# Attention and MLP on one core: turning q, k and the attention's rows by DMA instead of on TensorE

## The chip, the cores and the metric

The kernel runs on one NeuronCore of a Trainium2 chip. The metric is the device time of one execution in microseconds (us); times compared are medians of several runs. The engines are named as in the profile: PE is TensorE (matrix multiplication), PEld its weight loads, DVE is VectorE, ACT is ScalarE, POOL is GpSimd and SP is SyncE, which here only issues DMAs.

## The reference

Softmax attention over 8 batches, 12 heads, 448 positions, 64 columns per head; the heads' results stand side by side as rows of 768 columns; a two-layer MLP with a leaky ReLU follows.

```python
batch, n_heads, seq, head_dim = (8, 12, 448, 64)
scores = scale * np.matmul(q, k.transpose(0, 1, 3, 2))        # scale = 1 / sqrt(64)
attn = np.exp(scores - np.max(scores, axis=-1, keepdims=True))
attn = attn / (np.sum(attn, axis=-1, keepdims=True) + 1e-09)
attn_out = np.matmul(attn, v)
x = attn_out.transpose(0, 2, 1, 3).reshape(B * S, H * D)      # 3584 rows of 768
h = x @ w_in                                                  # w_in 768 x 2048
g = np.maximum(0.01 * h, h)
return g @ w_out                                              # w_out 2048 x 768
```

Inputs and output are float32; the kernel multiplies in bf16.

## The kernel before

Two heads make a **pair**; there are 48 pairs, numbered u, six in a batch. A pair's q, k and v are 448 rows, held as 112 partitions with four rows each (SC = 112, NSC = 4), two heads of 64 columns beside each other, so that a block of 112 partitions has 128 columns.

For each pair these functions run:

- `load(u)`: three DMAs from SP's queue bring q, k and v (224 KB each) into the buffers fq, fk, fv; the pool `ld` holds six pairs.
- `cast(u)`: POOL turns them into bf16: tiles q and k, and v into one of five v tiles.
- `transposes(u)`: eight PE transposes of 112 x 128 blocks (four of q, four of k) into the PSUM tile tr, and one DVE copy (L154) to qkT, of which there are three. qkT has the 128 columns of both heads on its partitions, and first q's, then k's 448 positions in the free dimension.
- `scores(u, c)`: two matmuls into PSUM (sc) for each of four groups of 112 keys; `expo(u, c)`: ACT's exponential to the tile e.
- `pv(u, j)`: sixteen matmuls for each head, with a column of ones in v that gives the sum; DVE divides (L188, L189) and writes bf16 rows x.
- `x_transposes(u)`: four PE transposes of x into tr and one or two DVE copies (L202) to xT, whose partitions are columns of the MLP's input and whose free dimension is its rows.

The MLP runs over eight groups of rows, `cuts` = 0, 384, 896, 1280, 1792, 2176, 2688, 3072, 3584, so widths of 384 and 512 alternate. A group's xT is a tile of its own (three in the pool); where a batch's 448 rows cross a cut, they are copied in two pieces. `mlp(i)` multiplies by w_in (96 matmuls, L225, with an activation on ACT to h, L230) and then by w_out (32 matmuls, L237, for each 128 rows, with DVE copies to o, L242, and two stores from SP). It is a generator that yields after each matmul.

The order is written out by hand: nothing is scheduled behind the program's back, each engine runs its instructions in the order of the program, and semaphore waits are set where an instruction needs another's result or buffer. A pair has eight slots s0 to s7 (`slots(u)`): s0 scores of u, s1 `x_transposes(u - 2)`, s2 and s6 pv of u - 1, s3 `load`, s4 scores, s5 `cast(u + 3)` and, early on, a piece of the weights' load on POOL's queue, s7 `transposes(u + 1)`. Between two slots matmuls of `mlp(i)` are put in proportion: `begin[i]` is the slot from which `mlp(i)` is dealt out until `begin[i + 1]`. Whatever is left of a group's MLP is run at its end, and the last group's MLP runs alone. So SP's queue also holds, in the program's order, loads and stores, and a store that waits for its o holds the loads behind it.

```python
begin = [8 * (HP * (i + 1) + 1) + 2 for i in range(B)]
```

Of the kernel before, what the change touches and what calls it, by code (L numbers as in the profile page):

```python
# [10 lines left out]
BF16 = mybir.dt.bfloat16  # L11
# [5 lines left out]
def kernel(  # L17
# [9 lines left out]
    nc = tc.nc  # L27

    B, H, S, D = q.shape
    DM, DF = moe_w_in.shape  # L30
    P = 128
    HP = H // 2
    SC = 112
    NSC = S // SC
    KD = DM // P
    MD = DF // P
    NW = DM // 2
    NU = B * HP
    scale = 1.0 / float(D) ** 0.5

    cuts = [((b * S) // P) * P for b in range(B)] + [B * S]
# [2 lines left out]

    const_pool = ctx.enter_context(tc.tile_pool(name="const", bufs=1))
    w_pool = ctx.enter_context(tc.tile_pool(name="weights", bufs=1))
    ld_pool = ctx.enter_context(tc.tile_pool(name="ld", bufs=6))
    cast_pool = ctx.enter_context(tc.tile_pool(name="cast", bufs=4))
    v_pool = ctx.enter_context(tc.tile_pool(name="vones", bufs=1))
    qk_pool = ctx.enter_context(tc.tile_pool(name="qk", bufs=1))  # L50
    exp_pool = ctx.enter_context(tc.tile_pool(name="exp", bufs=1))
    r_pool = ctx.enter_context(tc.tile_pool(name="rec", bufs=4))
    x_pool = ctx.enter_context(tc.tile_pool(name="x", bufs=3))
    xT_pool = ctx.enter_context(tc.tile_pool(name="xT", bufs=3))
    h_pool = ctx.enter_context(tc.tile_pool(name="h", bufs=2))
    o_pool = ctx.enter_context(tc.tile_pool(name="o", bufs=3))

# [11 lines left out]
    e_sb = [exp_pool.tile([SC, EL + P - SC], BF16, name=f"e{i}") for i in range(NE)]  # L69


    NQ = 3
    QL = 2 * S
    qkT = [qk_pool.tile([P, QL + P - SC], BF16, name=f"qkT{i}") for i in range(NQ)]

    w_in_sb = w_pool.tile([P, KD, DF], BF16)
    w_out_sb = w_pool.tile([P, MD, DM], BF16)
# [1 line left out]
    w_out_v = moe_w_out.rearrange("(ko ki) n -> ki ko n", ki=P)  # L79

    raw = {}
    q_sb = {}
    k_sb = {}

    def load(u, queues=(nc.sync,) * 3):
        if u >= NU:
            return
        b, hp = divmod(u, HP)  # L90
        raw[u] = []
        for a, name, eng in zip((q, k, v), ("fq", "fk", "fv"), queues):
            t = ld_pool.tile([SC, 2, NSC, D], F32, name=name)
            eng.dma_start(
                out=t.rearrange("p h so d -> p h (so d)"),
                in_=a[b, 2 * hp:2 * hp + 2].rearrange("h (p so) d -> p h (so d)", so=NSC),
            )
            raw[u].append(t)

    def cast(u, by=(nc.gpsimd.tensor_copy,) * 3):  # L100
        if u >= NU:
            return
        fq, fk, fv = raw.pop(u)
        q_sb[u] = cast_pool.tile([SC, NSC, 2, D], BF16, name="q")
        k_sb[u] = cast_pool.tile([SC, NSC, 2, D], BF16, name="k")
        by[0](q_sb[u].rearrange("p so h d -> p h so d"), fq)  # L106
        by[1](k_sb[u].rearrange("p so h d -> p h so d"), fk)  # L107
        by[2](v_sb[u % NV][:, :, :, :D], fv)  # L108

    w_steps = []  # L110
# [5 lines left out]
    def load_w(n=1):  # L116
        for _ in range(n):
            if w_steps:
                o, i = w_steps.pop(0)
                nc.gpsimd.dma_start(out=o, in_=i)  # L120

    load(0, (nc.sync, nc.scalar, nc.sync))
    for i in range(1, 6):
        load(i)
    ident = const_pool.tile([P, P], BF16)
    make_identity(nc, ident)
# [10 lines left out]


    x_t = {}
    xT = [None] * (B + 1)  # L140

    def get_xT(i):
        if xT[i] is None:
            xT[i] = xT_pool.tile([P, KD, 4 * P], BF16, name="xT")
        return xT[i]

    def transposes(u):
        tr = ps_tr.tile([P, 2, S], BF16, name="tr")
        for i, src in enumerate((q_sb[u], k_sb[u])):
            for so in range(NSC):  # L150
                nc.tensor.transpose(  # L151
                    tr[:, i, ts(so, SC)], src[:, so], ident[:SC, :SC]
                )
        nc.vector.tensor_copy(qkT[u % NQ][:, :QL], tr.rearrange("p i s -> p (i s)"))  # L154

    sc_t = {}

    def scores(u, c):
        ps = ps_s.tile([P, 2, 512], F32, name="sc")
        t = qkT[u % NQ]  # L160
        sc_t[u, c] = ps
        for j in range(2):
            nc.tensor.matmul(  # L163
                ps[:, j, :S],
                t[j * D:(j + 1) * D, S + c * SC:S + c * SC + P],
                t[j * D:(j + 1) * D, :S],
                start=True, stop=True,
            )

    def expo(u, c):  # L170
        e = e_sb[u % NE][:, :EL].rearrange("p (j c s) -> p j c s", j=2, c=NSC)
        nc.scalar.activation(e[:, :, c, :], sc_t.pop((u, c))[:SC, :, :S], AX.Exp, scale=scale)  # L172

    def pv(u, j):

        e, vt = e_sb[u % NE], v_sb[u % NV]
        ps = ps_pv.tile([P, NSC, D + 1], F32, name="pv")
        for qc in range(NSC):
            for c in range(NSC):
                at = (j * NSC + c) * S + qc * SC  # L180
                nc.tensor.matmul(  # L181
                    ps[:, qc, :], e[:, at:at + P], vt[:, j, c, :],
                    start=(c == 0), stop=(c == NSC - 1),
                )
        if j == 0:
            x_t[u] = x_pool.tile([SC, NSC, 2, D], BF16, name="x")
        rec = r_pool.tile([SC, NSC, 1], F32, name="rec")
        nc.vector.reciprocal(rec, ps[:SC, :, D:])  # L188
        nc.vector.tensor_mul(  # L189
            x_t[u][:, :, j, :], ps[:SC, :, :D], rec.to_broadcast([SC, NSC, D])  # L190
        )

    def x_transposes(u):
        b, hp = divmod(u, HP)
        lo, hi = b * S, (b + 1) * S
        tr = ps_tr.tile([P, 2, S], BF16, name="tr")
        for so in range(NSC):
            nc.tensor.transpose(tr[:, 0, ts(so, SC)], x_t[u][:, so], ident[:SC, :SC])  # L198
        for i in (b, b + 1):
            a, z = max(lo, cuts[i]), min(hi, cuts[i + 1] if i < B else hi)  # L200
            if a < z:
                nc.vector.tensor_copy(  # L202
                    get_xT(i)[:, hp, a - cuts[i]:z - cuts[i]], tr[:, 0, a - lo:z - lo]
                )
        del x_t[u]


    def store(o, t0):

        done = 0  # L210
        while done < P:
            b, j = divmod(t0 + done, S)
            so, p = divmod(j, SC)
            n = min(SC - p, P - done)
            dst = out[b * S:(b + 1) * S].rearrange("(p so) n -> so p n", so=NSC)
            nc.sync.dma_start(out=dst[so, p:p + n], in_=o[done:done + n, :])
            done += n

    def mlp(i):
        n = cuts[i + 1] - cuts[i]  # L220
        h = h_pool.tile([P, MD, 4 * P], BF16, name="h")
        for m in range(MD):
            ps = ps_mm.tile([P, 4 * P], F32, name="mm")
            for kk in range(KD):
                nc.tensor.matmul(  # L225
                    ps[:, :n], w_in_sb[:, kk, ts(m, P)], get_xT(i)[:, kk, :n],
                    start=(kk == 0), stop=(kk == KD - 1),
                )
                if kk == KD - 1:
                    nc.scalar.activation(h[:, m, :n], ps[:, :n], AX.Prelu, alpha=0.01)  # L230
                yield n
        for c in range(n // P):
            o = o_pool.tile([P, DM], F32, name="o")
            for w in range(2):
                ps = ps_mm.tile([P, 4 * P], F32, name="mm")
                for m in range(MD):
                    nc.tensor.matmul(  # L237
                        ps[:, :NW], h[:, m, ts(c, P)], w_out_sb[:, m, ts(w, NW)],
                        start=(m == 0), stop=(m == MD - 1),
                    )  # L240
                    if m == MD - 1:
                        nc.vector.tensor_copy(o[:, ts(w, NW)], ps[:, :NW])  # L242
                    yield NW
            store(o, cuts[i] + c * P)


    def slots(u):

        on = u < NU

        def s0():
            if on:
                scores(u, 0)
                scores(u, 1)
                expo(u, 0)

        def s1():
            if on:
                expo(u, 1)
            if 2 <= u <= NU + 1:  # L260
                x_transposes(u - 2)

        def s2():
            if 1 <= u <= NU:
                pv(u - 1, 0)

        def s3():
            load(u + 6)

        def s4():  # L270
            if on:
                scores(u, 2)
                scores(u, 3)
                expo(u, 2)

        def s5():
            if on:
                expo(u, 3)
            cast(u + 3)
            if u <= 2 or 5 <= u <= 8:  # L280
                load_w()

        def s6():
            if 1 <= u <= NU:
                pv(u - 1, 1)

        def s7():
            if u + 1 < NU:
                transposes(u + 1)

        return [s0, s1, s2, s3, s4, s5, s6, s7]

    steps = [s for u in range(NU + 2) for s in slots(u)]

    begin = [8 * (HP * (i + 1) + 1) + 2 for i in range(B)]
    assert begin[B - 1] == 8 * (NU + 1) + 2
    transposes(0)
    for s in steps[:begin[0]]:
        s()
    for i in range(B):  # L300
        work = steps[begin[i]:begin[i + 1]] if i + 1 < B else []
        n = cuts[i + 1] - cuts[i]
# [42 lines left out]
```

## Time and profile before

| | |
|---|---|
| median of three runs | 460.23 us (457.93 to 462.13) |
| profiled execution, its own time | 456.92 us |
| its span, first to last instruction | 455.2 us |
| granted TensorE clock, mean | 0.998 |
| PE, ACT, DVE, POOL busy | 95%, 51%, 30%, 20% of the span |
| HBM read and written | 45.61 MB and 11.01 MB |
| PE transposes | 576 in three groups: q and k (L151), x (L198) |

Lines such as L151 are lines of the kernel before. A row of a group reads: line, engine, operation, tile written <- tiles read, shapes, count, then busy time in us and the mean duration of one in ns, then the idle time of the engine ahead of it and what ended that. A row of the timeline has the start and the length in us first. In the chain, shares are of the span.

### The profile page before, as it was taken

How to read it: one execution, taken by the hardware profiler on the slowest of the kernel's cores; microseconds unless marked ns; L12 is line 12 of the kernel's file. 1: busy time of each engine (PE TensorE's matmuls, PEld its weight loads, DVE VectorE, ACT ScalarE, POOL GpSimd, SP SyncE). 2: the span in 40 equal slices, each digit the busy share in tenths (PEclk: the TensorE clock that was granted, in tenths of full speed). 3: DMA queues.
4: the chain of work that ended last, by engine and by line, in shares of the span. 5: the costliest groups of instructions: out<-in, count | busy, mean ns of one | idle time of the engine just before them, and what ended most of it. 6: DMA issues, size and time to landing. Idle time of an engine off the chain costs nothing.

```text
span 455.2 us, 9874 instructions
## 1 busy us (share of the span) xinstructions
PE 433.2 (95%) x4143; PEld 248.0 (54%) x4160; DVE 137.8 (30%) x369; ACT 230.6 (51%) x322; POOL 92.1 (20%) x167
## 2 busy tenths in 40 slices
PE   3878999999999999999999999999999999999995
PEld 1545555544556566555555665554556655564463
DVE  1344224422333333332233322342233423340021
ACT  4677663467434675446634476446644376404300
POOL 5536423111221121131111211311221100000000
PEclk9999999999999999999999999999999999999999
DMA  9999996391043810565024460349004110111022
GB/s 233 253 245 275 239 252 189 98 239 39 1 131 97 230 49 1 159 182 133 1 81 127 127 171 2 96 125 249 1 1 131 36 37 2 35 37 35 1 69 69
DMA packets 44332, 50.97 MB, mean 112 GB/s; under 512 B 3328, under 2 KB 40704, under 8 KB 44288
## 3 DMA queue, kind: packets, MB, share of 16 engines
q1 hardware_dynamic: 38800, 43.82, 35.2%
q0 software_dynamic: 5248, 6.29, 7.8%
q8 instruction: 32, 0.52, 0.5%
q10 hardware_dynamic: 240, 0.23, 0.2%
q14 instruction: 12, 0.10, 0.1%
HBM read 45.61 MB, written 11.01 MB: 124 GB/s over the span
## 4 chain that ended last, share of the span: by engine, by line
PE 82%; DMA 13%; DVE 3%; ACT 1%; issue 1%; POOL 0%; POOLq 0%; SPq 0%
PE mm L237 31%; PE mm L225 28%; PE pv L181 9%; PE sc L163 9%; DMA w_out_sb<-in_moe_w_out_dram 4%; PE tr L151 4%; DMA fq<-in_q_dram 4%; DMA fk<-in_k_dram 3%; DVE qkT L154 3%; PE tr L198 2%; DMA fv<-in_v_dram 2%; ACT e L172 1%; POOL v L108 0%; DVE o L242 0%; DVE q L106 0%
## 5 line engine op out<-in xcount | busy, mean ns | idle before, releaser
L172 ACT ACTIVATE e<-sc 112x896 bf16<-112x896 f32 x192 | 167.9, 915 | 126.5 <-PE sc L163 126.2
L237 PE MATMUL mm<-w_out_sb,h 128*128 128x384 bf16 x896 | 166.2, 326 | 0.5 <-DMA w_out_sb<-in_moe_w_out_dram 0.5
L225 PE MATMUL mm<-xT,w_in_sb 128*128 128x384 bf16 (+1 forms) x751 | 164.5, 352 | 0.9
L237 PEld LDWEIGHTS <-h 128*128 128x128 bf16 x896 | 79.5, 97 | 57.9 <-issue 15.1
L230 ACT ACTIVATE h<-mm 128x384 bf16<-128x384 f32 (+1 forms) x128 | 69.8, 545 | 69.7 <-PE mm L225 69.7
L225 PEld LDWEIGHTS <-w_in_sb 128*128 128x128 bf16 x768 | 66.7, 97 | 63.9 <-issue 15.6
L108 POOL CAST v<-fv 112x512 bf16<-112x512 f32 x48 | 29.6, 616 | 239.5 <-PE pv L181 225.9
L181 PEld LDWEIGHTS <-e 112*128 112x128 bf16 x1536 | 62.2, 99 | 15.2 <-issue 1.5
L163 PE MATMUL sc<-qkT 64*128 64x448 bf16 x384 | 56.3, 367 | 10.9 <-DVE qkT L154 6.5
L181 PE MATMUL pv<-v,e 112*128 112x65 bf16 x1536 | 66.2, 195 | 0.0
L242 DVE COPY o<-mm 128x384 f32<-128x384 f32 x56 | 31.2, 557 | 96.8 <-PE mm L237 96.8
L188 DVE RECIPROCAL rec<-pv 112x4 f32<-112x4 f32 x96 | 17.5, 182 | 114.2 <-PE pv L181 114.0
L189 DVE TENSOR_TENSOR x<-pv,rec 112x256 bf16<-112x256 f32 x96 | 40.7, 424 | 3.3
L202 DVE COPY xT<-tr 128x384 bf16<-128x384 bf16 (+1 forms) x72 | 20.3, 309 | 70.9 <-PE tr L198 70.9
L154 DVE COPY qkT<-tr 128x896 bf16<-128x896 bf16 x48 | 29.9, 622 | 23.6 <-PE tr L151 23.5
L163 PEld LDWEIGHTS <-qkT 64*128 64x128 bf16 x384 | 12.1, 95 | 44.5 <-DVE qkT L154 24.7
L106 POOL CAST q<-fq 112x512 bf16<-112x512 f32 x47 | 28.9, 614 | 22.7 <-POOL v L108 13.2
L107 POOL CAST k<-fk 112x512 bf16<-112x512 f32 x47 | 28.9, 614 | 12.8 <-DMA fk<-in_k_dram 9.6
L151 PE MATMUL tr<-ident,q 112*128 112x112 bf16 x192 | 17.9, 217 | 4.8 <-DVE q L106 4.8
L151 PEld LDWEIGHTS <-q 112*128 112x128 bf16 x192 | 14.0, 99 | 11.3 <-DVE q L106 4.8
L198 PEld LDWEIGHTS <-x 112*128 112x128 bf16 x192 | 13.8, 98 | 9.0 <-issue 2.6
L151 PE MATMUL tr<-ident,k 112*128 112x112 bf16 x192 | 17.9, 218 | 0.0
(16 smaller groups left out, 40.1 us busy)
## 6 DMA issues: line engine op xcount, KB each, us to landing
fq<-in_q_dram SPq DMA_DIRECT2D x48, 224.0 KB, 5.5
fv<-in_v_dram SPq DMA_DIRECT2D x48, 224.0 KB, 6.0
fk<-in_k_dram SPq DMA_DIRECT2D x47, 224.0 KB, 6.1
w_in_sb<-in_moe_w_in_dram POOLq DMA_DIRECT2D x4, 768.0 KB, 12.7
w_out_sb<-in_moe_w_out_dram POOLq DMA_DIRECT2D x4, 768.0 KB, 15.9
out_dram<-o SPq DMA_DIRECT2D x8, 336.0 KB, 2.9
out_dram<-o SPq DMA_DIRECT2D x8, 288.0 KB, 2.7
out_dram<-o SPq DMA_DIRECT2D x8, 240.0 KB, 2.7
```

The source lines that it names most:

```text
L106: by[0](q_sb[u].rearrange("p so h d -> p h so d"), fq)
L108: by[2](v_sb[u % NV][:, :, :, :D], fv)
L151: nc.tensor.transpose(tr[:, i, ts(so, SC)], src[:, so], ident[:SC, :SC])
L154: nc.vector.tensor_copy(qkT[u % NQ][:, :QL], tr.rearrange("p i s -> p (i s)"))
L163: nc.tensor.matmul(ps[:, j, :S], t[j * D:(j + 1) * D, S + c * SC:S + c * SC + P], t[j * D:(j + 1) * D, :S], start=True, stop=True,)
L172: nc.scalar.activation(e[:, :, c, :], sc_t.pop((u, c))[:SC, :, :S], AX.Exp, scale=scale)
L181: nc.tensor.matmul(ps[:, qc, :], e[:, at:at + P], vt[:, j, c, :], start=(c == 0), stop=(c == NSC - 1),)
L189: nc.vector.tensor_mul(x_t[u][:, :, j, :], ps[:SC, :, :D], rec.to_broadcast([SC, NSC, D]))
L225: nc.tensor.matmul(ps[:, :n], w_in_sb[:, kk, ts(m, P)], get_xT(i)[:, kk, :n], start=(kk == 0), stop=(kk == KD - 1),)
L230: nc.scalar.activation(h[:, m, :n], ps[:, :n], AX.Prelu, alpha=0.01)
L237: nc.tensor.matmul(ps[:, :NW], h[:, m, ts(c, P)], w_out_sb[:, m, ts(w, NW)], start=(m == 0), stop=(m == MD - 1),)
L242: nc.vector.tensor_copy(o[:, ts(w, NW)], ps[:, :NW])
```

## The change

Pairs 0 to 9 still have q and k turned on PE, and pairs 0 to 6 their x. For the others an SP-issued transposing DMA moves the rows from SBUF to SBUF: one for q and k together, which now stand in one tile qkb, and one for x. The q/k DMA of pair u + 2 is issued in slot s1 of pair u, right behind the x DMA of pair u - 2. There are four qkT instead of three. xT becomes one tile of 4 x 448 = 1792 columns in which four batches follow each other, so a batch's rows are written in one piece. The pool `ld` holds five pairs, and `load` runs five pairs ahead. The MLP of groups 1 to 7 begins five slots later (s7 in place of s2); that of group 0 begins as before and so is dealt out over 53 slots instead of 48.

```diff
-    ld_pool = ctx.enter_context(tc.tile_pool(name="ld", bufs=6))
+    ld_pool = ctx.enter_context(tc.tile_pool(name="ld", bufs=5))
...
-    NQ = 3
+    NQ = 4
...
+    NX = 4 * S
+    xT = xT_pool.tile([P, KD, NX], BF16)
...
-        q_sb[u] = cast_pool.tile([SC, NSC, 2, D], BF16, name="q")
-        k_sb[u] = cast_pool.tile([SC, NSC, 2, D], BF16, name="k")
+        qk_sb[u] = cast_pool.tile([SC, 2, NSC, 2, D], BF16, name="qkb")
...
+    NPE = 10
+
+    def turn(dst, src):
+        nc.sync.dma_start_transpose(out=dst.rearrange("p (c s) -> p c s", s=SC), in_=src)
+
+    def dma_transposes(u):
+        if NPE <= u < NU:
+            turn(qkT[u % NQ][:, :QL], qk_sb[u].rearrange("p i so h d -> p (i so h d)"))
+
     def transposes(u):
+        if u >= min(NPE, NU):
+            return
...
     def x_transposes(u):
         b, hp = divmod(u, HP)
+        at = b * S % NX
+        dst = xT[:, hp, at:at + S]
+        if u >= NPE - 3:
+            turn(dst, x_t.pop(u).rearrange("p so h d -> p (so h d)"))
+            return
...
-                    ps[:, :n], w_in_sb[:, kk, ts(m, P)], get_xT(i)[:, kk, :n],
+                    ps[:, :n], w_in_sb[:, kk, ts(m, P)], xT[:, kk, at:at + n],
...
             if 2 <= u <= NU + 1:
                 x_transposes(u - 2)
+            dma_transposes(u + 2)
...
-            load(u + 6)
+            load(u + 5)
...
-    begin = [8 * (HP * (i + 1) + 1) + 2 for i in range(B)]
+    begin = [8 * (HP * (i + 1) + 1) + 7 - 5 * (i == 0) for i in range(B)]
```

The first place is PE's order where the last pair ends and the last group's MLP begins. Before, x of pair 47 was turned (L198) four matmuls ahead of it; LDWEIGHTS rows are the weight loads of the matmul that follows:

```order
L237 LDWEIGHTS h
L237 MATMUL mm<-w_out_sb,h 128x384
L198 LDWEIGHTS x
L198 MATMUL tr<-ident,x 128x112
...
L237 LDWEIGHTS h
L237 MATMUL mm<-w_out_sb,h 128x384
...
L225 LDWEIGHTS w_in_sb
L225 MATMUL mm<-xT,w_in_sb 128x512
```

And now, behind the last pv of pair 47:

```order
L189 LDWEIGHTS e_112
L189 MATMUL pv<-v_107,e_112 128x65
L244 LDWEIGHTS h
L244 MATMUL mm<-w_out_sb,h 128x384
...
L232 LDWEIGHTS w_in_sb
L232 MATMUL mm<-xT,w_in_sb 128x512
```

The transposes are gone from PE's order, and 36 matmuls of the MLP of group 6 (L244) stand between the last pv and the last group's first matmul (L232).

The second place is SP's queue at the first transposing DMAs. Before, behind the three loads of pair 12, only loads followed for four pairs (in brackets the semaphores that an instruction waits for: DMAHW is a DMA eight places earlier in the queue):

```order
L94 DMA fq<-in_q_dram 112x2x256 [waits DMAHW7_49,Pool_49]
L94 DMA fk<-in_k_dram 112x2x256 [waits DMAHW0_49,Pool_49]
L94 DMA fv<-in_v_dram 112x2x256 [waits DMAHW1_49,Pool_49]
L94 DMA fq<-in_q_dram 112x2x256 [waits DMAHW2_49,Pool_49]
L94 DMA fk<-in_k_dram 112x2x256 [waits DMAHW3_49,Pool_49]
L94 DMA fv<-in_v_dram 112x2x256 [waits DMAHW4_49,Pool_49]
```

And now:

```order
L147 DMA_TRANSPOSE qkT_115<-qkb 128x8x112 [waits DVE_49,DMAHW7_49,PE_49,Pool_49]
L98 DMA fq<-in_q_dram 112x2x256 [waits DMAHW0_49]
L98 DMA fk<-in_k_dram 112x2x256 [waits DMAHW1_49]
L98 DMA fv<-in_v_dram 112x2x256 [waits DMAHW2_49]
L147 DMA_TRANSPOSE xT<-x 128x4x112 [waits DMAHW3_49,DVE_49]
L147 DMA_TRANSPOSE qkT_116<-qkb 128x8x112 [waits DMAHW4_49,PE_49,Pool_49]
L98 DMA fq<-in_q_dram 112x2x256 [waits DMAHW5_49]
```

The loads of pair 13 now stand behind the DMA of q and k of pair 10, which waits for that pair's casts on POOL and for the scores of pair 6 on PE; those of pair 14 stand behind the DMA of x of pair 7, which waits for DVE.

The third place is SP's queue near the end, from the store of the second 128 rows' result of group 6 on. Before:

```order
L216 DMA out_dram<-o 96x768 [waits DMAHW4_49,DVE_49]
L216 DMA out_dram<-o 32x768 [waits DMAHW5_49]
L216 DMA out_dram<-o 80x768 [waits DMAHW6_49,DVE_49]
L216 DMA out_dram<-o 48x768 [waits DMAHW7_49]
L216 DMA out_dram<-o 64x768 [waits DMAHW0_49,DVE_49]
```

And now:

```order
L222 DMA out_dram<-o 96x768 [waits DMAHW2_49,DVE_49]
L222 DMA out_dram<-o 32x768 [waits DMAHW3_49]
L147 DMA_TRANSPOSE xT<-x 128x4x112 [waits DMAHW4_49]
L222 DMA out_dram<-o 80x768 [waits DMAHW5_49,DVE_49]
L222 DMA out_dram<-o 48x768 [waits DMAHW6_49]
```

The DMA of x of pair 47 stands behind two stores, the first of which waits for DVE's copy of a result, and ahead of the store of the third 128 rows.

More of the change, by code (lines that the diff above doesn't have):

```diff
@@ L53 @@
     x_pool = ctx.enter_context(tc.tile_pool(name="x", bufs=3))
-    xT_pool = ctx.enter_context(tc.tile_pool(name="xT", bufs=3))
+    xT_pool = ctx.enter_context(tc.tile_pool(name="xT", bufs=1))
     h_pool = ctx.enter_context(tc.tile_pool(name="h", bufs=2))
@@ L69 @@
     e_sb = [exp_pool.tile([SC, EL + P - SC], BF16, name=f"e{i}") for i in range(NE)]
-    NQ = 3
+    NQ = 4
     QL = 2 * S
     qkT = [qk_pool.tile([P, QL + P - SC], BF16, name=f"qkT{i}") for i in range(NQ)]
+    NX = 4 * S
+    assert all(any(c == d for d in cuts) for c in range(0, B * S + 1, NX))
+    xT = xT_pool.tile([P, KD, NX], BF16)
     w_in_sb = w_pool.tile([P, KD, DF], BF16)
@@ L81 @@
     raw = {}
-    q_sb = {}
-    k_sb = {}
+    qk_sb = {}
     def load(u, queues=(nc.sync,) * 3):
@@ L103, in cast @@
         fq, fk, fv = raw.pop(u)
-        q_sb[u] = cast_pool.tile([SC, NSC, 2, D], BF16, name="q")
-        k_sb[u] = cast_pool.tile([SC, NSC, 2, D], BF16, name="k")
-        by[0](q_sb[u].rearrange("p so h d -> p h so d"), fq)
-        by[1](k_sb[u].rearrange("p so h d -> p h so d"), fk)
+        qk_sb[u] = cast_pool.tile([SC, 2, NSC, 2, D], BF16, name="qkb")
+        by[0](qk_sb[u][:, 0].rearrange("p so h d -> p h so d"), fq)
+        by[1](qk_sb[u][:, 1].rearrange("p so h d -> p h so d"), fk)
         by[2](v_sb[u % NV][:, :, :, :D], fv)
@@ L122 @@
     load(0, (nc.sync, nc.scalar, nc.sync))
-    for i in range(1, 6):
+    for i in range(1, 5):
         load(i)
@@ L139 @@
     x_t = {}
[L140 to L145, printed above, removed]
+    NPE = 10
[4 more added lines that the diff above has]
+            turn(qkT[u % NQ][:, :QL], qk_sb[u].rearrange("p i so h d -> p (i so h d)"))
     def transposes(u):
+        if u >= min(NPE, NU):
+            return
         tr = ps_tr.tile([P, 2, S], BF16, name="tr")
-        for i, src in enumerate((q_sb[u], k_sb[u])):
+        for i in range(2):
             for so in range(NSC):
                 nc.tensor.transpose(
-                    tr[:, i, ts(so, SC)], src[:, so], ident[:SC, :SC]
+                    tr[:, i, ts(so, SC)], qk_sb[u][:, i, so], ident[:SC, :SC]
                 )
@@ L194, in x_transposes @@
         b, hp = divmod(u, HP)
-        lo, hi = b * S, (b + 1) * S
+        at = b * S % NX
[3 more added lines that the diff above has]
+            return
         tr = ps_tr.tile([P, 2, S], BF16, name="tr")
@@ L198, in x_transposes @@
             nc.tensor.transpose(tr[:, 0, ts(so, SC)], x_t[u][:, so], ident[:SC, :SC])
[L199 to L205, printed above, removed]
+        nc.vector.tensor_copy(dst, tr[:, 0, :])
     def store(o, t0):
@@ L220, in mlp @@
         n = cuts[i + 1] - cuts[i]
+        at = cuts[i] % NX
         h = h_pool.tile([P, MD, 4 * P], BF16, name="h")
@@ L293 @@
     steps = [s for u in range(NU + 2) for s in slots(u)]
-    begin = [8 * (HP * (i + 1) + 1) + 2 for i in range(B)]
-    assert begin[B - 1] == 8 * (NU + 1) + 2
+    begin = [8 * (HP * (i + 1) + 1) + 7 - 5 * (i == 0) for i in range(B)]
+    assert begin[B - 1] == 8 * (NU + 1) + 7
     transposes(0)
```

## The prediction

> **What bounds the kernel now.** I read the page from the top: the busy shares, the slices, the chain that ended last.
>
> ```profile
> span 455.2 us, 9874 instructions
> PE 433.2 (95%) x4143; PEld 248.0 (54%) x4160; DVE 137.8 (30%) x369; ACT 230.6 (51%) x322; POOL 92.1 (20%) x167
> DMA  9999996391043810565024460349004110111022
> PE 82%; DMA 13%; DVE 3%; ACT 1%; issue 1%; POOL 0%; POOLq 0%; SPq 0%
> ```
>
> TensorE (PE) is busy for 95% of the span. The DMA engines, in the second line from below, a digit for each slice of 11.4 us, are full for six slices (68 us) and lightly used afterwards. Busy time by stage confirms it (columns: window, then PE, PEld, DVE, ACT, POOL, then granted clock, DMA share, GB/s):
>
> ```profile
> 50.00:60.00 10.00, 9.93 (x97) 5.59 (x96) 2.23 (x6) 7.33 (x13) 2.46 (x4) 1.00 1.14 239
> 90.00:149.00 59.00, 58.73 (x549) 32.48 (x551) 18.54 (x52) 29.42 (x41) 10.73 (x18) 1.00 0.37 98
> 149.00:198.00 49.00, 48.54 (x505) 28.83 (x504) 16.54 (x44) 27.68 (x40) 10.72 (x18) 1.00 0.39 110
> ```
>
> In these windows PE is idle for less than 1% of the time. So an instruction taken off PE shortens the kernel by the time until PE's next one starts, as long as nothing else becomes late. In these stages DMA stands at 0.37 to 0.39 of its capacity and ACT at about half.
>
> **What PE gives up.** The price is the pitch, not the duration. First two groups by shape:
>
> ```profile
> L151 PE MATMUL tr<-ident,q 112*128 112x112 bf16 x192 | 17.9, 217 | 4.8 <-DVE q L106 4.8
> L198 PE MATMUL tr<-ident,x 112*128 112x112 bf16 x192 | 17.6, 215 | 0.0
> ```
>
> Then PE's timeline inside one pair (start, length, what):
>
> ```profile
> 203.00 0.36 PE L151 MATMUL tr<-ident,q 112*128 112x112 bf16 x4
> 203.20 0.36 PE L151 MATMUL tr<-ident,k 112*128 112x112 bf16 x4
> 203.40 1.03 PE L225 MATMUL mm<-xT,w_in_sb 128*128 128x512 bf16 x3
> 204.36 0.55 PE L163 MATMUL sc<-qkT 64*128 64x448 bf16 x4
> ...
> 205.72 0.36 PE L198 MATMUL tr<-ident,x 112*128 112x112 bf16 x4
> 205.91 1.03 PE L225 MATMUL mm<-xT,w_in_sb 128*128 128x512 bf16 x4
> ...
> 214.07 0.55 PE L163 MATMUL sc<-qkT 64*128 64x448 bf16 x4
> ```
>
> A transpose lasts 215 ns, but the first of k starts 0.20 us after the first of q, and the MLP's matmul 0.20 us after that: the eight of q and k occupy PE for 0.40 us (50 ns each), and the four of x for 0.19 us (205.72 to 205.91). The change takes q and k of pairs 10 to 47 off PE, 38 x 0.40 = 15.2 us, and x of pairs 7 to 47, 41 x 0.19 = 7.8 us: **23.0 us** in all, and none of it lies beside other PE work. The groups' busy time (53 us for all transposes) would promise 43 us; it counts pipeline overlap with the neighbours and is not what goes.
>
> DVE loses the copies out of PSUM (L154, L202); at 30% busy they were not on the path: 0. The longer distance of the MLP's start (five slots later from batch 1 on) moves work between slots and adds none: 0, since PE has MLP work queued in every slot.
>
> **What is late next.** A long pair runs 9.71 us from one group of scores to the same one of the next (204.36 to 214.07). A short one (MLP width 384) runs 8.14:
>
> ```profile
> 54.63 0.55 PE L163 MATMUL sc<-qkT 64*128 64x448 bf16 x4
> ...
> 62.77 0.55 PE L163 MATMUL sc<-qkT 64*128 64x448 bf16 x4
> ```
>
> After the change they take 9.12 and 7.55 us, 8.34 in the mean. The next engine is ACT:
>
> ```profile
> L172 ACT ACTIVATE e<-sc 112x896 bf16<-112x896 f32 x192 | 167.9, 915 | 126.5 <-PE sc L163 126.2
> L230 ACT ACTIVATE h<-mm 128x384 bf16<-128x384 f32 (+1 forms) x128 | 69.8, 545 | 69.7 <-PE mm L225 69.7
> L242 DVE COPY o<-mm 128x384 f32<-128x384 f32 x56 | 31.2, 557 | 96.8 <-PE mm L237 96.8
> ```
>
> Four exponentials at 915 ns and 16/6 activations of the MLP at 545 make 5.1 us of ACT a pair; it does not become the bound. (The third row serves below.) What is new is on the DMA side, and nothing in this trace shows a transposing DMA, so I bound it.
>
> *Transfer time.* A pair's q and k are 112 x 1024 bf16 = 224 KB, its x 112 KB. In blocks of 128 columns a source row has 256 B, so a pair has 896 + 448 = 1344 pieces, 84 per DMA engine.
>
> ```profile
> q1 hardware_dynamic: 38800, 43.82, 35.2%
> q8 instruction: 32, 0.52, 0.5%
> fq<-in_q_dram SPq DMA_DIRECT2D x48, 224.0 KB, 5.5
> out_dram<-o SPq DMA_DIRECT2D x8, 144.0 KB, 2.5
> out_dram<-o SPq DMA_DIRECT2D x8, 48.0 KB, 2.1
> ```
>
> On q1 a packet of 1.13 KB costs 0.352 x 16 x 455.2 / 38800 = 66 ns; on q8 one of 16 KB costs 0.005 x 16 x 455.2 / 32 = 1.14 us. That is about 70 ns per KB in both, so time goes by bytes and hardly by the packet. By bytes a piece costs 17 ns, 84 pieces 1.4 us a pair; by the packet 84 x 66 = 5.5 us. The loads take 672 / 16 x 66 = 2.8 us a pair and the stores (3584 rows of 3 KB, 198 ns each) 3584 / 48 / 16 x 0.198 = 0.9. The sum is 5.1 or 9.2 us, beside 8.34 of PE. I take 1.4 us, for which the two rows speak: hidden. [...]
>
> *Latency of q and k.* The DMA for pair u+2 is issued in step u, two steps (15 us) before its scores. The landing lies between 2.1 us and the 5.5 us of a load: 0.
>
> *Latency of x.* Inside the kernel x of a batch's last pair has eight slots, a pair's time, before its MLP starts. The last batch is tightest:
>
> ```profile
> 405.40 0.68 PE L181 MATMUL pv<-v,e 112*128 112x65 bf16 x16
> 406.33 0.42 DVE L189 TENSOR_TENSOR x<-pv,rec 112x256 bf16<-112x256 f32 x1
> 429.60 20.81 PE mm L237 x128
> ```
>
> x is ready 0.7 us after the last pv ends (406.75 against 406.08). In the new order 36 output matmuls follow that pv, 36 x 20.81/128 = 5.9 us, and the five first matmuls of each group read other pairs' rows, another 1.1. SP first waits for four of these matmuls (0.65 us) and their result's copy (0.56), and issues two stores (0.41 each, below): 2.0 us, so 4.9 us are left for the landing of 112 KB. The nearest store, 144 KB, took 2.5: 0. Ends: 0, and 2 us at each of seven batches if it lands like a slow load, 14 us.
>
> *SP's queue.* SP works in order. Behind a transpose that waits for x or for a cast stand the loads of pair u+5 and the stores. A load now goes out once per step, and its cast comes two and a half steps later.
>
> ```profile
> POOL v L108 <- PE pv L181: 225.9, 34, 7.5
> 53.37 2.47 SPq L94 DMA_DIRECT2D fq<-in_q_dram  x1
> 95.19 0.41 SPq L94 DMA_DIRECT2D fq<-in_q_dram  x1
> 95.69 0.41 SPq L94 DMA_DIRECT2D fk<-in_k_dram  x1
> ```
>
> POOL waits for PE and not for loads, so one buffer fewer costs 0; without that cover a load late by its landing would cost 5.5 us. Issuing a load of 224 pieces takes 0.41 us in a quiet stage; 1344 pieces at that rate are 2.5 us, with loads and stores 4.2 us of SP a pair: hidden.
>
> *The crowded stage.* First and last of twelve loads in SP's timeline, and PE's wait for the last quarter of w_out, which lands just in time:
>
> ```profile
> 44.12 1.01 SPq L94 DMA_DIRECT2D fq<-in_q_dram  x1
> ...
> 65.45 0.31 SPq L94 DMA_DIRECT2D fv<-in_v_dram  x1
> 68.45 0.81 PE L237 MATMUL mm<-w_out_sb,h 128*128 128x384 bf16 x4 [0.46 <-DMA w_out_sb<-in_moe_w_out_dram]
> ```
>
> Between 44 and 68 us SP starts the loads of four pairs (13 to 16). Held by its new waits it will start three, and 3 x 224 + 2 x 112 = 896 KB of transposes: 224 KB more net, 0.9 us at the 239 GB/s of that stage. Without the relief it would be 3.8 us; since the first MLP is spread over 53 slots instead of 48, its second half also comes a little later, and it may be 0. I take **+1**.
>
> **Sum.** The profiled execution took 456.9 us (span 455.2). 456.9 - 23.0 + 1 = 434.9. The median shown is 460.2, 3.3 above it; the same 22 us off that give 438.2. I say 436, between the two.
>
> **Rivals.** (1) *It lands late*: x at the starts of batches and w_out at 68 us, up to 14 + 3.8 us, 438 to 453. For it: no row shows this operation's latency. Against: 7.5 us of slack in six batches and 4.9 in the last, beside landings of 2.5 us in the nearest row.
>
> (2) *The DMA engines become the bound*, slower: at 66 ns for each 256 B piece a pair costs them 9.2 us against 8.34, from about 48 us on; 434.9 + 38 x 0.86 = 468. It begins to hurt at 46 ns a piece (short pairs) and ends above the median from 63 ns. Against it stand the two queue rows.
>
> (3) *SP's issue becomes the bound*: at the crowded rate, 2.47 us for 224 pieces, 1344 pieces take 14.8 us, with the rest 16.5 a pair; 434.9 + 38 x 8.2 = 745. Those rates are seen only while the DMA share is above 1.1.
>
> (4) *The blocks go one behind another*, each at the landing floor of 2.1 us: 12 x 2.1 = 25 us a pair, 434.9 + 38 x 16.9 = 1077. Against it: three loads of 5.5 us each are issued 0.5 us apart, and their landings overlap. [...]
>
> **Chances.** Forecast (431 to 438) 0.66, rival 1 0.13, rival 2 0.12, rival 3 0.06, rival 4 0.03. The range leaves out rivals 2 to 4: from 431 (no loss at w_out, 433.9, less the 2 us by which single runs lie apart from their median) to 453. About 1% (4.6 us) is what a measurement here can tell from no change. Faster takes the forecast and most of rival 1, 0.77; same the rest of it and a mild rival 2, 0.06; slower 0.17.
>
> **What would show it.** Right: PE's pairs at 9.1 and 7.5 us between the same scores, PE idle below 1% after 70 us, DMA share between 0.5 and 0.7 in the middle, landings below 6 us. Rival 2 shows as a DMA share near 1 throughout and PE waiting for qkT; rival 3 as SP's issues lasting over 4 us; rival 1 as idle time before L232 ended by a DMA of xT, or before L244 by w_out. The sum would be wrong if the granted clock fell below 1.00 with PE fuller, which no row excludes.

## The result and the profile after

The changed kernel takes 437.4 us (median of four runs, 436.2 to 439.1), the kernel before 459.5 in the same comparison: a ratio of 0.952, 95% interval 0.946 to 0.957. The forecast of 436 was 1.4 us off. The profiled execution took 439.14 us, the slowest of the four; its span is 437.3 against 455.2. Lines such as L147 are from here on those of the changed kernel; two experiments that add lines shift them.

The page of the changed kernel, its busy shares, slices, chain and main DMA queue:

```profile
span 437.3 us, 8922 instructions
PE 411.6 (94%) x3692; PEld 226.0 (52%) x3692; DVE 98.0 (22%) x266; ACT 230.1 (53%) x322; POOL 91.1 (21%) x168
PEclk9999997999999999999999999999999999999999
DMA  9999999976556675676466665598456540130022
PE 83%; DMA 15%; issue 0%; POOL 0%; DVE 0%; SPq 0%; POOLq 0%
q1 hardware_dynamic: 93744, 57.25, 56.0%
```

PE lost 21.6 us of busy time and is still the bound. The DMA engines now stay between four and nine tenths through the middle. Two things are new: in the first quarter a slice in which the clock granted to PE is 0.7, and a larger share of DMA in the chain, 15% for 13%. Busy time by stage (same columns as before the change):

```profile
60.00:70.00 10.00, 3.97 (x30) 1.71 (x27) 0.61 (x2) 2.16 (x5) 2.21 (x4) 0.76 1.16 216
90.00:149.00 59.00, 59.00 (x505) 30.49 (x504) 12.64 (x35) 31.90 (x44) 11.46 (x20) 1.00 0.65 148
149.00:198.00 49.00, 49.00 (x473) 27.68 (x471) 11.80 (x33) 29.25 (x43) 12.04 (x21) 1.00 0.69 167
```

In the windows from 70 to 390 us PE has no idle time left. Between 60 and 70 us it works 4 us of 10. PE's timeline there:

```profile
59.76 0.68 PE L189 MATMUL pv<-v,e 112*128 112x65 bf16 x16
60.27 1.30 PE L232 MATMUL mm<-xT,w_in_sb 128*128 128x384 bf16 x7
67.60 0.93 PE L171 MATMUL sc<-qkT 64*128 64x448 bf16 x4 [6.03 <-DMA qkT<-qkb]
68.46 2.42 PE L232 MATMUL mm<-xT,w_in_sb 128*128 128x384 bf16 x7
70.68 1.08 PE L189 MATMUL pv<-v,e 112*128 112x65 bf16 x16
71.58 1.64 PE L232 MATMUL mm<-xT,w_in_sb 128*128 128x384 bf16 x8
73.14 0.55 PE L171 MATMUL sc<-qkT 64*128 64x448 bf16 x4
```

The list of waits has it as one case (total, times, longest):

```profile
PE sc L171 <- DMA qkT<-qkb: 6.0, 1, 6.0
```

PE waits 6.03 us for q and k of pair 10, the first that come by DMA. After that pause seven matmuls take 2.42 us where they took 1.30 before it, and sixteen of pv 1.08 where they took 0.68. From 67.60 to 73.14 some 2.0 us more go than the same instructions need elsewhere (5.54 against 0.48 + 1.15 + 0.51 + 1.40, the distances between the same rows at full clock). So this place costs **8.0 us** in the profiled execution. SP's timeline shows where it comes from:

```profile
47.09 7.56 SPq L147 DMA_TRANSPOSE qkT<-qkb  x1
54.72 0.56 SPq L98 DMA_DIRECT2D fq<-in_q_dram  x1
...
59.36 5.55 SPq L147 DMA_TRANSPOSE xT<-x  x1
65.02 3.87 SPq L147 DMA_TRANSPOSE qkT<-qkb  x1
...
71.65 1.19 SPq L147 DMA_TRANSPOSE xT<-x  x1
73.39 1.22 SPq L147 DMA_TRANSPOSE qkT<-qkb  x1
```

The list of DMA issues shows what is usual (count, median us to landing):

```profile
xT<-x SPq DMA_TRANSPOSE x41, 2.6
qkT<-qkb SPq DMA_TRANSPOSE x38, 3.0
```

Issued at 47.09, this DMA keeps SP for 7.56 us, and the pause ends 20.5 us after its start. In a quiet stage the same thing takes SP 1.2 us and lands in 3.0. For the rest of the kernel the pairs run as forecast or better. A short pair, then a long one, each from its first scores to the next pair's:

```profile
163.18 0.55 PE L171 MATMUL sc<-qkT 64*128 64x448 bf16 x4
...
170.59 0.55 PE L171 MATMUL sc<-qkT 64*128 64x448 bf16 x4
...
201.31 0.55 PE L171 MATMUL sc<-qkT 64*128 64x448 bf16 x4
...
210.42 0.55 PE L171 MATMUL sc<-qkT 64*128 64x448 bf16 x4
```

7.41 us and 9.11 us; 7.55 and 9.12 were forecast.

### The profile page after: what moved, and what is told of

Its sections match the earlier page's. It is cut to its first block, busy times and chain, and to the rows that moved or that the text cites. A ratio compares the mean times of both kernels' runs of the same rounds, so it can differ in the third digit from the quotient of the medians.

```text
span 437.3 us, 8922 instructions
## 1 busy us (share of the span) xinstructions
PE 411.6 (94%) x3692; PEld 226.0 (52%) x3692; DVE 98.0 (22%) x266; ACT 230.1 (53%) x322; POOL 91.1 (21%) x168
## 4 chain that ended last, share of the span: by engine, by line
PE 83%; DMA 15%; issue 0%; POOL 0%; DVE 0%; SPq 0%; POOLq 0%
PE mm L244 34%; PE mm L232 31%; PE pv L189 9%; PE sc L171 9%; DMA fk<-in_k_dram 5%; DMA qkT<-qkb 5%; DMA fq<-in_q_dram 3%; DMA fv<-in_v_dram 2%; POOL qkb L110 0%; DVE o L249 0%; SPq L98 0%; POOLq L109 0%; POOL v L111 0%
## 5 line engine op out<-in xcount | busy, mean ns | idle before, releaser
L232 PE MATMUL mm<-xT,w_in_sb 128*128 128x384 bf16 (+1 forms) x768 | 162.7, 355 | 0.0
L244 PE MATMUL mm<-w_out_sb,h 128*128 128x384 bf16 x896 | 160.2, 326 | 0.0
L244 PEld LDWEIGHTS <-h 128*128 128x128 bf16 x896 | 81.7, 98 | 62.4 <-issue 14.1
L232 PEld LDWEIGHTS <-w_in_sb 128*128 128x128 bf16 x768 | 68.9, 98 | 71.6 <-issue 17.3
L109 POOL CAST qkb<-fq 112x512 bf16<-112x512 f32 x47 | 28.9, 614 | 27.2 <-DMA qkT<-qkb 14.1
L110 POOL CAST qkb<-fk 112x512 bf16<-112x512 f32 x47 | 28.9, 614 | 9.8 <-DMA fk<-in_k_dram 9.6
L159 PE MATMUL tr<-ident,qkb 112*128 112x112 bf16 x80 | 6.9, 238 | 5.0 <-DVE qkb L109 5.0
L159 PEld LDWEIGHTS <-qkb 112*128 112x128 bf16 x80 | 5.2, 111 | 5.9 <-DVE qkb L109 5.0
L162 DVE COPY qkT<-tr 128x896 bf16<-128x896 bf16 x10 | 6.2, 620 | 6.0 <-PE tr L159 5.9
L211 DVE COPY xT<-tr 128x448 bf16<-128x448 bf16 x7 | 2.7, 392 | 7.9 <-PE tr L210 7.9
L123 POOL DMA_DIRECT2D w_in_sb<-in_moe_w_in_dram x4 | 3.4, 852 | 0.0
L210 PEld LDWEIGHTS <-x 112*128 112x128 bf16 x28 | 1.7, 102 | 2.7 <-issue 2.6
## 6 DMA issues: line engine op xcount, KB each, us to landing
w_in_sb<-in_moe_w_in_dram POOLq DMA_DIRECT2D x4, 768.0 KB, 13.6
```

What stands on the lines that cost most here:

```text
L109: by[0](qk_sb[u][:, 0].rearrange("p so h d -> p h so d"), fq)
L110: by[1](qk_sb[u][:, 1].rearrange("p so h d -> p h so d"), fk)
L232: nc.tensor.matmul(ps[:, :n], w_in_sb[:, kk, ts(m, P)], xT[:, kk, at:at + n], start=(kk == 0), stop=(kk == KD - 1),)
L244: nc.tensor.matmul(ps[:, :NW], h[:, m, ts(c, P)], w_out_sb[:, m, ts(w, NW)], start=(m == 0), stop=(m == MD - 1),)
```

## Experiments

Theory A: the gain is what PE's transposes cost in pitch, on every pair; one stall in the crowded stage before 70 us takes a third of it back, because w_out and the loads fill the DMA engines. Rivals: the first transposing DMA is slow in itself (B); the other parts of the change bring the gain (C); the new DMAs stand close to a bound of their own (2 and 3 of the prediction). Medians, with the ratio to the kernel before and its 95% interval (two runs for half of w_out, ten for the two kernels with all on PE, four for the others):

| kernel | us | ratio | interval |
|---|---|---|---|
| the change | 437.4 | 0.952 | 0.946 to 0.957 |
| all on PE, the rest of the change | 459.0 | 1.000 | 0.998 to 1.002 |
| q and k alone by DMA | 445.6 | 0.971 | 0.968 to 0.974 |
| x alone by DMA | 449.8 | 0.981 | 0.978 to 0.983 |
| DMA from pair 14 | 435.4 | 0.948 | 0.944 to 0.952 |
| half of w_out not loaded | 431.0 | 0.942 | 0.937 to 0.947 |
| w_out sooner | 436.1 | 0.951 | 0.946 to 0.956 |
| each transposing DMA twice, from pair 14 | 436.1 | 0.953 | 0.951 to 0.956 |
| all on PE, two slots earlier | 455.2 | 0.994 | 0.991 to 0.996 |
| from pair 12, PE's two slots earlier | 435.1 | 0.951 | 0.946 to 0.956 |
| from pair 14, two slots earlier | 435.0 | 0.946 | 0.938 to 0.953 |
| from pair 14, w_out sooner | 434.5 | 0.946 | 0.939 to 0.953 |
| from pair 14, two slots earlier, w_out sooner | 430.0 | 0.937 | 0.933 to 0.942 |

The runs belong to five comparisons, in which the medians of the kernel before lie between 458.1 and 459.6 us. So a difference of about 1 us between two rows shows nothing.

### Which part brings the gain

All on PE:

```diff
-    NPE = 10
+    NPE = NU + 3
```

> All pairs are turned on PE, and everything else of the change stays (ring, five load buffers, four qkT, one tile for q and k, MLP groups five slots later). Theory A (the gain comes from PE's transposes): as before the change, 457 to 461 us. Rival C (the gain comes from the other parts, the ring's undivided copies or the later groups): 437 to 445 us.

459.0 us, no change within 0.2%. The ring, the undivided copies, the five load buffers and the later groups together are worth nothing; rival C is out.

q and k alone (in `x_transposes`, x always on PE), then x alone (no DMA for q and k, `transposes` always on PE):

```diff
-        if u >= NPE - 3:
+        if u >= NU:
```

> q and k by DMA from pair 10 as in the change, x always on PE. Theory A: 41 x 0.19 = 7.8 us come back, the wait for qkT of pair 10 stays: about 445 us. If the x transposes in the queue caused that wait, it is gone and the time is about 437 us.

```diff
-        if NPE <= u < NU:
+        if False:
...
-        if u >= min(NPE, NU):
+        if u >= NU:
```

> x by DMA from pair 7 as in the change, q and k always on PE. Theory A: 7.8 us less than before the change and no wait in the crowded stage, since x of pair 7 is wanted only at 90 us: about 451.5 us. Rival C: 437 to 445 us.

445.6 and 449.8 us: gains of 13.4 and 9.2 on 459.0, together 22.6, and the change has 21.6 on the same 459.0. The second is 1.7 us more than expected. Period for period the two parts add up: a long pair takes 9.72 us with all on PE, 9.52 with x by DMA (0.20 off), 9.32 with q and k by DMA (0.40 off) and 9.11 with both. The wait for pair 10 is there without any x in the queue, 3.67 us in that profile, so it does not take x to cause it. Whether x adds the 2.4 us by which the change's wait is longer, one profile of each does not show:

```profile
65.39 0.93 PE L171 MATMUL sc<-qkT 64*128 64x448 bf16 x4 [3.67 <-DMA qkT<-qkb]
```

### What makes the first one late

```diff
-    NPE = 10
+    NPE = 14
```

> The DMA transposes begin at pair 14 (q, k) and 11 (x) instead of 10 and 7. Theory A (the 6 us for which PE waits for qkT of pair 10 come from the crowded stage, in which w_out and the loads fill the DMA engines): the first transposing DMA goes out after 70 us, is issued in about 1.2 us and lands in about 3, and PE waits for none; minus 8.0 us (6.0 idle and 2.0 at a lower clock behind it), plus 4 x 0.6 us of PE transposes that come back and some 0.5 us of waits for DVE's copies: about 432 us. Rival B (the first transposing DMA is slow in itself, wherever it comes): the wait of 6 us moves to pair 14 and the time is 439 to 441.

435.4 us; the forecast of theory A was 432. There is no wait for qkT in the profile: the first transposing DMA goes out at 77 us, is issued in 1.45 us, and the slowest of all 34 lands in 4.7. SP's timeline, and the landings of qkT (min/median/max):

```profile
77.37 1.45 SPq L147 DMA_TRANSPOSE qkT<-qkb  x1
```

```profile
DMA to landing us min/median/max: 2.9/3.0/4.7
```

Rival B is out. The time is 3 us above the forecast. The two profiled spans differ by 3.9 us (437.3 and 433.4) where 5.1 were expected, and the PE timelines show why. Beside the first MLP a pair turned by DMA takes 6.92 us (the change, first two lines) and one turned on PE 7.82 (all on PE, last two):

```profile
76.53 0.55 PE L171 MATMUL sc<-qkT 64*128 64x448 bf16 x4
...
83.45 0.55 PE L171 MATMUL sc<-qkT 64*128 64x448 bf16 x4
```

```profile
45.84 0.55 PE L171 MATMUL sc<-qkT 64*128 64x448 bf16 x4 [0.23 <-DVE qkT L162]
...
53.66 0.55 PE L171 MATMUL sc<-qkT 64*128 64x448 bf16 x4 [0.23 <-DVE qkT L162]
```

So four pairs back on PE cost 3.6 us and not 2.9. And the first MLP matmul came 0.6 us later (41.85 for 41.28), behind a granted clock of 0.96 between 0 and 40 us, where the change has 1.00; sixteen of pv take 1.09 us for 0.68 at 32 us. The medians differ by 2.0 only. The stall was sized in the slowest of the change's executions (439.1 of 436.2 to 439.1); all four have the same mean clock, 0.992, but whether PE's pause was shorter in the other three stays open, since they have no trace.

To take the crowd away instead, two of w_out's four loads were left out:

```diff
-    for i in range(4):
+    nc.vector.memset(w_out_sb[:, MD // 2:, :], 0.0)
+    for i in range(2):
         w_steps.append((w_out_sb[...], w_out_v[...]))
```

> The change with two of the four loads of w_out left out; its second half is set to zero by DVE at the start, so the output lacks that half's part. Theory A (the first transposing DMA is late because w_out and the loads fill the DMA engines up to 68 us): with 3 MB less to read the crowded stage ends some 12 us earlier, q and k of pair 10 are issued in under 4 us and land in under 10, PE does not wait for them: 428 to 432 us. If it is slow for another reason the wait of 4 to 6 us stays: 436 to 439 us.

431.0 us, no wait for qkT. SP's timeline at the same DMA, and its landings:

```profile
45.59 5.34 SPq L148 DMA_TRANSPOSE qkT<-qkb  x1
```

```profile
DMA to landing us min/median/max: 2.9/3.0/13.6
```

It is still issued slowly (5.34 us, not under 4) and the slowest landing is 13.6 us, not under 10, but that is in time. So with less data in flight both are shorter (5.34 for 7.56 us and 13.6 for 20.5), as theory A has it, and here that was enough, though the stage did not become quiet (DMA share 1.13 between 60 and 70 us). Moving w_out's loads ahead without leaving any out does not help:

```diff
-            if u <= 2 or 5 <= u <= 8:
+            if u <= 6:
                 load_w()
```

> The change with the four loads of w_out issued two pairs sooner (in the steps of pairs 3 to 6 instead of 5 to 8), nothing left out. Theory A (what is late up to 70 us is decided by the order in which a full DMA system serves w_out, the loads and the first transposes): w_out is done by about 60 us, the loads that follow have three pairs of lead to give, q and k of pair 10 land before PE wants them at 61: 430 to 434 us. If the lead is too small, casts and scores wait for loads before 60 us and the time is 436 to 440 us.

436.1 us, a miss of theory A's figure and the second case of the expectation. The transposing DMA now goes out at 55.82, because the loads ahead of its casts are late in w_out's place, and PE waits 3.46 us for it at the same point:

```profile
55.82 4.96 SPq L147 DMA_TRANSPOSE qkT<-qkb  x1
...
64.93 0.93 PE L171 MATMUL sc<-qkT 64*128 64x448 bf16 x4 [3.46 <-DMA qkT<-qkb]
```

Up to some 70 us the DMA engines are full in both orders (share 1.16 in the change and 1.18 here between 60 and 70 us). What was early becomes late in exchange.

### Are the new DMAs close to a bound

```diff
-    NPE = 10
+    NPE = 14
...
+            turn(again[:, 0, :], qk_sb[u].rearrange("p i so h d -> p (i so h d)"))
...
+            turn(again[:, 1, :S], x)
```

Each copy stands right behind the real one and goes to a tile that nobody reads.

> As from pair 14, but each transposing DMA is issued twice, the second time into a tile that nobody reads. Theory A (transfer and issue are hidden behind PE): SP issues 4.8 us of transposes, 1.4 of loads and 0.5 of stores in a short pair of 7.4, the DMA share rises from 0.60 to about 0.85, and the time stays within 2 us of 435.4. Rivals 2 and 3 of the prediction (DMA engines or SP's issue close to being the bound): pairs of 8 us and more, above 445 us.

436.1 us, 0.8 above the single ones by the medians (by the ratios, 0.953 and 0.948, some 2.5). The DMA share of the windows goes to 0.90, and the main queue carries 49312 packets more than with single ones:

```profile
150.00:350.00 200.00, 198.02 (x1783) 107.22 (x1791) 44.50 (x124) 113.83 (x161) 43.11 (x71) 1.00 0.90 190
```

```profile
q1 hardware_dynamic: 137424, 67.93, 71.0%
```

Twice the transposes still fit behind PE; only two pairs at the starts of MLP groups became 0.7 and 1.1 us longer, and there PE waits 0.47 and 0.96 us for a DMA of x. So rivals 2 and 3 had room for twice the transposes, at a share of 0.90; for more than that no run shows it.

### The waits for DVE's copies

In the change, short pairs lose 0.73 us, 0.14 more than the transposes' pitch. With all on PE, the scores of a short pair start 0.88 us after four matmuls that need 0.65:

```profile
175.54 0.81 PE L244 MATMUL mm<-w_out_sb,h 128*128 128x384 bf16 x4
176.42 0.55 PE L171 MATMUL sc<-qkT 64*128 64x448 bf16 x4
```

They wait for DVE's copy of qkT; beside the first MLP the same kernel's timeline names that wait (0.23 us before the scores at 45.84, 53.66 and 61.48 us, ended by DVE qkT). To test that, PE's transposes were put two slots earlier, with everything on PE:

```diff
         def s5():
...
+            if u + 1 < NU:
+                transposes(u + 1)
             cast(u + 3)
...
         def s7():
-            if u + 1 < NU:
-                transposes(u + 1)
+            pass
```

> All pairs turned on PE, two slots earlier than before. Theory A (a short pair loses 0.13 us more than the transposes' pitch because its scores wait for DVE's copy): the wait goes, short pairs fall from 8.14 to about 8.0 us, long ones stay at 9.72, and the attention alone gains up to 4 us: 452 to 456 us, against 459.0. Rival D (that 0.13 us has another cause, the grouping of the MLP's matmuls): pairs as before, 457 to 460 us.

455.2 us. Short pairs take 8.01 us, long ones stay at 9.72, as expected (the same scores of two pairs in a row are the first and the third line):

```profile
171.97 0.55 PE L171 MATMUL sc<-qkT 64*128 64x448 bf16 x4
176.07 0.55 PE L171 MATMUL sc<-qkT 64*128 64x448 bf16 x4
...
179.98 0.55 PE L171 MATMUL sc<-qkT 64*128 64x448 bf16 x4
```

Rival D is out: what is left between 8.01 and the change's 7.41 is the pitch, 0.59. So the waits for copies were part of what the change removed. Here too PE waits for w_out, 2.75 us at 69 us, which takes back part of what the attention alone gained.

### Towards a better version

The same two slots together with DMA from pair 12:

> DMA transposes from pair 12 (q, k) and 9 (x), and the PE transposes of the pairs before them two slots earlier, so that DVE's copy is done when the scores come. Theory A: against 435.4 us from pair 14, 2 x 0.75 us fewer on PE and some 1.2 us fewer waits for copies beside the MLP, and up to 3.6 us where the attention runs alone (0.87 us of waiting in each of its pairs): 429 to 433 us, without a wait for qkT of pair 12. If the stage up to 70 us is too crowded for pair 12, a wait of some us shows there and the time is 435 to 440 us.

435.1 us, above the range of theory A and in the second case of the expectation, though what is late is not qkT. The pairs of the attention alone fall from 4.49 to 3.83 us and the first MLP matmul comes at 37.9 us in place of 41.3, but PE then waits for w_out instead, 4.66 us, and its clock falls again behind it (0.66 between 70 and 80 us):

```profile
71.68 0.48 PE L244 MATMUL mm<-w_out_sb,h 128*128 128x384 bf16 x1 [4.66 <-DMA w_out_sb<-in_moe_w_out_dram]
```

This is the crowded stage once more (DMA share 1.16 between 60 and 70 us): time gained ahead of it is given back in it. The four executions lie between 432.7 and 437.6 us, with a mean clock of 0.996 and 0.999 in the two shorter ones and 0.988 in the two longer, so the loss is not the same in each. From pair 14 the remedies were then tried one by one and together. The earlier slots alone:

> DMA transposes from pair 14 and PE's transposes two slots earlier, w_out in its old place. Theory A: the 3 to 4 us won in the attention alone are given back in a wait for w_out between 66 and 72 us and a lower clock behind it: 433 to 437 us. If the earlier slot alone is enough: 429 to 432 us and no wait for w_out.

435.0 us: the gain of the attention alone goes into a wait for w_out, 2.66 us, and slower matmuls behind it (sixteen of pv take 1.09 us for 0.68; the mean clock of this execution is 0.991, and 0.996 from pair 14 alone), as theory A has it:

```profile
69.08 0.32 PE L244 MATMUL mm<-w_out_sb,h 128*128 128x384 bf16 x1 [2.66 <-DMA w_out_sb<-in_moe_w_out_dram]
...
72.07 1.09 PE L189 MATMUL pv<-v,e 112*128 112x65 bf16 x16
```

w_out sooner alone:

> DMA transposes from pair 14 and w_out two pairs sooner, PE's transposes in their old slot. Theory A: w_out was not late from pair 14 on, so its earlier load brings nothing by itself: 434 to 436 us, as from pair 14 alone. If it is the order of w_out that made the fastest version fast: 429 to 432 us.

434.5 us: nothing that the runs can tell, since w_out was not late there. And all three (pair 14, two slots earlier, w_out two pairs sooner):

> DMA transposes from pair 14, PE transposes before them two slots earlier, and w_out's loads two pairs sooner: the three remedies together. Theory A: the attention-alone stage keeps its 3 to 4 us (first MLP matmul at 38 instead of 41 us), PE does not wait for w_out at 66 to 72 us, no wait for qkT: 427 to 431 us. If the first 70 us are bound by the bytes that must arrive, the gain is given back in waits for loads or w_out: 433 to 437 us, as from pair 14 alone.

430.0 us, 0.937 of before (0.933 to 0.942): the fastest of all. PE is busy for ten of ten, in the crowded stage too:

```profile
50.00:60.00 10.00, 10.00 (x111) 5.92 (x109) 3.33 (x9) 6.93 (x12) 3.14 (x5) 1.00 1.14 248
60.00:70.00 10.00, 10.00 (x114) 6.26 (x113) 3.39 (x10) 6.50 (x9) 6.14 (x10) 1.00 1.12 263
70.00:80.00 10.00, 10.00 (x104) 5.84 (x103) 3.54 (x10) 4.61 (x6) 4.23 (x7) 1.00 1.00 234
```

Neither of the two later remedies does it alone (435.0 and 434.5). With no transposing DMA before 74 us, w_out first and the loads afterwards, nothing that PE wants between 40 and 70 us comes late.

## Why the prediction was right

- *PE's transposes cost their pitch, 23.0 us*: right. The periods of the single parts show 0.40 us for q and k and 0.20 for x.
- *Latency of q and k: 0*: this step failed. It bounded the landing by rows of stores and loads from a whole-kernel list (2.1 to 5.5 us) and gave it 15 us of slack; in the crowded stage the first one took 20.5. The stall belongs to rival 1, but at qkT, not at x or w_out.
- *The crowded stage: +1*: mis-sized. It costs 8.0 us in the profiled execution, 6.0 of waiting and 2.0 at a lower clock, a thing the sum had no term for. The wait for w_out at 68 us (0.46) is gone, since PE arrives later.
- *DVE's copies: 0*: mis-sized the other way. Short pairs fell by 0.73 us (8.14 to 7.41), and beside the first MLP by 0.90 (7.82 with all on PE, 6.92 now), where the transposes' pitch is 0.59: their scores no longer wait for a copy. From the first MLP matmul (40.85 before, 41.28 after) to the last group's first (408.94 and 390.88) the kernel lost 18.5 us. 23.0 for the transposes and 0.5 for w_out, less 8.0, leave 3.0, and by estimate some twenty short pairs at 0.14 to 0.3 us make that up.
- *Transfer time: 1.4 us a pair, between 1.4 and 5.5*: q1 carried 54944 packets and 13.43 MB more (244 B each), where 52416 pieces of 256 B were counted, and q1's time grew by 0.560 x 16 x 437.3 - 0.352 x 16 x 455.2 = 1355 us of one engine for them: 25 ns a packet, 2.1 us a pair, if loads and stores cost what they did before. Nearer to the lower bound, and hidden. The 17 ns of the sum came from "about 70 ns per KB in both" rows; they give 58 (66 / 1.13) and 71 (1.14 us / 16), and neither led to 25. The second copies cost 24 ns each (1189 us for 49312).
- *SP's issue: 2.5 us a pair*: 2.4, but as 1.2 for each DMA, of 224 KB as of 112 KB, not by pieces.
- *Latency of x and the buffers: 0*: right; x lands in 2.6 us by the median (13.2 at most), and the last group's first matmul follows without a gap.

Of the signs that it named, the pairs' periods and PE's idle time held, and the DMA share was 0.55 to 0.74 in the middle; landings below 6 us did not hold, and the clock did fall below 1.00 once. Two mistakes of opposite sign, a stall priced 7 us too low and a gain 3 us too low, let the forecast come closer than its terms, so that it missed by 1.4 us only is in part luck; the profiled execution is 4.2 us above the sum of 434.9. The regular part was sized from rows of the same stage; both errors lie where a stage or a pair differs from the one the row was taken from: the landing from medians of the whole kernel, and the transposes' pitch from a long pair, where no score waits for the copy.

By the engines' time, 244 B in 24.7 ns on 16 engines are an estimated 158 GB/s here. The eight blocks of q and k landed in 3.0 us by the median, and a pair's twelve took 2.1 us of the engines, so the blocks do not go one behind another at 2.1 us each (16.8 for eight), as rival 4 had it. For this kernel, with PE busy for 95% of the span, moving the transposes to DMA brought a ratio of 0.952.

## What to carry to other kernels

On a full engine, price an operation by the distance to the next instruction's start (0.20 us for four transposes here, of which one lasts 215 ns), in each kind of stage, and add the waits that its helper (here DVE's copy, 0.14 us in a short pair) puts on that engine. A DMA that moves work off the bound engine cost nothing here where the DMA engines had room (shares of 0.55 to 0.74); its first uses had to come after the stage in which they are full (1.13 to 1.19), and in that stage gains elsewhere were given back until the order of the transfers was right too. Test the capacity by issuing the new transfers twice: that one kernel showed room for twice the transposes (share 0.90).

## What the runs showed of the hardware

- A transposing DMA between SBUF tiles keeps SP for 1.2 us in a quiet stage, for four blocks as for eight, and lands in 2.6 and 3.0 us. With the DMA engines full (share 1.13 to 1.19, between 40 and 70 us), the issue took up to 7.6 us and the landing 20.5; between 71 and 80 us, in a window with a share of 1.23, the issue took 1.2 us again; in the run with DMA from pair 12 one issue took 10.6.
- After PE had paused for 6 us, its matmuls took about twice as long for some 4 us (granted clock 0.50 between 65.1 and 71.9 us, which makes 0.76 and 0.90 in the two windows of 10 us), so a pause of 6 us cost 8. Shorter pauses were followed by slower matmuls too: 2.75 us (all on PE, two slots earlier; PE resumed at 69.25, and the clock was 1.00 between 60 and 70 us and 0.83 between 70 and 80) and 2.66 us (from pair 14, two slots earlier); behind both, sixteen of pv took 1.09 us for 0.68. A pause of 1.45 us (each transposing DMA twice) left it at 1.00 between 70 and 80 us. From what length of a pause the clock falls these runs do not show: in the run from pair 14 sixteen of pv took 1.09 us at 32 us, with no pause above 0.9 us since 20 us.
